# The second batch's attention moved ahead of most of the first batch's blocks, in a strided-attention and two-layer expert kernel

## Chip, cores and metric

One core of a Trainium2 chip runs the whole program once. The metric is device time in microseconds of that core.

## What is computed

```python
scores = scale * np.matmul(q, k.transpose(0, 1, 3, 2))     # 2 batches, 8 heads, 576 positions, 64 wide
mask_local = (rel >= 0) & (rel < 32)                       # heads 0 to 3
mask_strided = (rel >= 0) & (pos[None, :] % 32 == pos[:, None] % 32)   # heads 4 to 7
attn = softmax(np.where(masks, scores, -1e9))
x = (attn @ v)                                             # reshaped to 1152 tokens x 512
x = ((x @ w1) * (x @ w2)) @ w3 @ w_out                     # 512 -> 1024 -> 1024 -> 512
out = sum(p[:, e:e + 1] * (np.maximum(x @ e1[e], 0) @ e2[e]) for e in range(4))
```

## The kernel before

Matrices that TensorE multiplies are kept as a high and a low part, and a product is three matmuls (`mm3`, lines 247 to 249: high by high, low by high, high by low). The order of all instructions is written out by hand; each engine works through its own list in order.

**Attention** of one batch is six chunks, three local and three strided (`Chunk4`), taken in nine pipelined steps by `attend(b, s)`. In step s TensorE makes the scores of chunk s (lines 323 and 328, or 332 and 339), VectorE takes maxima and subtracts (345, 348), ScalarE exponentiates (354). VectorE sums and normalises chunk s - 1 (360 to 365). TensorE transposes chunk s - 2 (370), ScalarE evacuates it (375). TensorE multiplies chunk s - 3 by the values (387, 396), ScalarE writes x_hi (`put`, line 423) and VectorE x_lo (`put_lo`, line 427). In the first batch `keep_warm(12)` (line 118) puts twelve idle matmuls behind each step.

**Blocks.** `ab_block(b, ft, n)` computes one unit: half a batch (288 tokens) by 128 columns of both w1 and w2. That is two accumulators of 24 matmuls together; ScalarE copies the first (444), VectorE multiplies by the second (446), ScalarE and VectorE split the product into ab_hi and ab_lo (448, 450). There are 2 batches x 8 column groups x 2 halves = 32 units, and `units` lists them in order. Accumulators, transposes and outputs of the values share a pool of five PSUM banks (`ps`); scores have three of their own.

**Weights** come as 64-bit words in 20 chunks of 1 MB (8 of w1 and w2, 4 of w_out, 8 of w3), through two raw buffers. A generator, `work()`, converts one chunk in four steps that `advance(n)` takes one by one: clamp (147) with the split of the chunk before on ScalarE (164); split on VectorE (174) and shift (150); ScalarE's conversion of the next raw chunk (136) and the sign (153); ScalarE's magnitude of the next (144) and the add (157). Behind the add the raw buffer is free and SP issues the next load (`load_next`, line 132). `live` counts the 16 tiles that values and converted chunks share; a w1/w2 chunk gives its two back when the second half of the second batch has used it.

**Order before.** The first batch's nine steps run alone, with two worker steps at the end of each from step 4 on. Then come the first batch's 16 units, each with two worker steps, and behind nine of them one step of the second batch's attention. Then come the second batch's 16 units, and behind them the product of w3 with w_out (`wc_tile`), the product with the blocks and the experts, none of which the change touches.

Of the kernel before, what the change touches and what calls it, by code (L numbers as in the profile page):

```python
# [16 lines left out]
B, H, S, D = 2, 8, 576, 64  # L17
# [25 lines left out]
def kernel(  # L43
# [148 lines left out]
    def load_next():  # L192
        nonlocal loaded
        if loaded < len(stream):
            stream[loaded].raw_load()
            loaded += 1
# [40 lines left out]
    def advance(n=1):  # L237

        return all([next(worker, False) for _ in range(n)])

    def need(c, part=0):
        while not (c.done if part == 0 else c.done1 if part == 1 else c.done2):
            assert advance()
# [12 lines left out]
    def load_qk(b, g, cut=0):  # L256

        tq, tk = (big[b].tile([P, 2, S], F32, tag="big", name=name) for name in ("tq", "tk"))
        pairs = slice(2 * g, 2 * g + 2)
        for c in ([slice(0, cut), slice(cut, S)] if cut else [slice(0, S)]):  # L260
            for t, src, queue in ((tk, kT, nc.sync), (tq, qT, nc.scalar if cut else nc.sync)):
                queue.dma_start(out=t[:, :, c], in_=src[b, pairs, :, c].rearrange("k p n -> p k n"))
        qk[b, g] = (tq, tk)

    def load_v_loc(b, c):

        tv = wp.tile([P, 2, 3, P], F32, tag="w", name="tv_loc")

        def load(dst, rows, t0, n):
            nc.sync.dma_start(out=dst, in_=v_loc[b, :, rows, t0:t0 + n].rearrange("k p t d -> p k t d"))  # L270

        lower, upper, middle = slice(0, 64), slice(64, P), slice(W, 3 * W)
        if c == 0:
            load(tv[lower, :, 0:1], lower, 0, 1)
            load(tv[upper, :, 0:1], middle, 0, 1)
            load(tv[:, :, 1:], slice(0, P), 1, 2)
        elif c == 1:
            load(tv, slice(0, P), 3, 3)
        else:
            load(tv[lower, :, 0:1], lower, 0, 1)  # L280
            load(tv[upper], middle, 3, 3)
            load(tv[lower, :, 1:], middle, 1, 2)
        vals[b, 0, c] = tv

    def load_v_str(b):

        threes = [wp.tile([P, n, P], F32, tag="w", name="tv_str") for n in (8, 4)]
        for tv, t0, n in ((threes[0], 0, 4), (threes[1], 4, 1)):
            for k in range(2):
                nc.sync.dma_start(out=tv[64 * k:64 * k + T3, :2 * n].rearrange("p (h t) d -> p h t d", h=2),  # L290
                                in_=v_str[b, k, :2 * T3, t0:t0 + n].rearrange("(h p) t d -> p h t d", h=2))
        for k in range(2):
            nc.sync.dma_start(out=threes[1][64 * k:64 * k + NB, 2:], in_=v_str[b, k, 2 * T3:2 * T3 + NB, :2])
        vals[b, 1] = threes
# [137 lines left out]
    def ab_block(b, ft, n):  # L432
        t = slice(b * S + n * HB, b * S + n * HB + HB)
        if n == 0 and ft % 2 == 0:
            ab_hi[b, ft // 2] = big[b].tile([P, 2, S], F32R, tag="big", name="ab_hi")
            ab_lo[b, ft // 2] = big[b].tile([P, 2, S], F32R, tag="big", name="ab_lo")
        hi, lo = (x[b, ft // 2][:, ft % 2, n * HB:n * HB + HB] for x in (ab_hi, ab_lo))
        ab = tmp.tile([P, HB], F32, tag="pT", name="ab")
        for w in range(2):
            acc = bank("ab_acc")[:, :HB]  # L440
            for k in range(4):
                mm3(acc, c_w12[ft].parts((w * 4 + k) * P, P), (x_hi[:, k, t], x_lo[:, k, t]), k == 0, k == 3)
            if w == 0:
                nc.scalar.copy(ab, acc)
            else:
                nc.vector.tensor_tensor(out=ab, in0=acc, in1=ab, op=ALU.mult)
            yield
        nc.scalar.copy(hi, ab)
        yield
        nc.vector.tensor_tensor(out=lo, in0=ab, in1=hi.bitcast(F32), op=ALU.subtract)  # L450
        yield
# [224 lines left out]
    def load_probs():  # L676
        den = const.tile([P, NTT], F32, name="den")
        nc.sync.dma_start(out=pn, in_=probs)
        nc.vector.tensor_reduce(out=den, in_=pn, axis=mybir.AxisListType.X, op=ALU.add)
        nc.vector.tensor_scalar_add(den, den, 1e-9)  # L680
        nc.vector.reciprocal(den, den)
        nc.vector.tensor_tensor(out=pn, in0=pn, in1=den.unsqueeze(2).to_broadcast([P, NTT, E]), op=ALU.mult)
# [4 lines left out]
    with tc.manual_schedule():  # L687
# [9 lines left out]
        strided_masks()  # L697
        load_v_loc(0, 0)
        load_qk(0, 1)
        load_next()  # L700
        load_v_loc(0, 1)
        load_v_loc(0, 2)
        load_v_str(0)
        load_next()
        load_qk(1, 0)
        for c in range(3):
            load_v_loc(1, c)
        chunks = [[Chunk4(3 * g + c, b, g, c) for g in range(2) for c in range(3)] for b in range(B)]
        units = [(b, ft, i) for b in range(B) for ft in range(8) for i in range(2)]
        done = 0  # L710

        rest = iter(())
# [1 line left out]
        def run_unit():  # L714

            nonlocal done, rest
            b, ft, i = units[done]
            need(c_w12[ft])
            block = ab_block(b, ft, i)
            for _ in range(2):  # L720
                next(rest, None)
                next(block)
                advance(1)
            rest = block
            done += 1
            if b == i == 1:
                c_w12[ft].free()

        def attend(b, s):

            nonlocal live
            chunk = chunks[b]
            n = len(chunk)
            if s < n:
                chunk[s].scores()
                chunk[s].maxima()
                chunk[s].exps()
            if 1 <= s <= n:
                chunk[s - 1].sums()
                chunk[s - 1].normalise()  # L740
            if 2 <= s < n + 2:
                chunk[s - 2].transposes()
                chunk[s - 2].evac(nc.scalar.copy)
            if 3 <= s:
                c = chunk[s - 3]
                c.pv()
                c.put()
                c.put_lo()
                if c.g == 0 or c.c > 0:
                    live -= 1  # L750

        for s in range(9):
            attend(0, s)
            keep_warm(12)
            if s > 3:
                advance(2)
        load_qk(1, 1)
        load_v_str(1)
        steps = iter(range(9))
        while done < 16:  # L760
            run_unit()
            if done in (2, 4, 5, 7, 8, 10, 11, 13, 14):
                attend(1, next(steps))
        load_probs()
        while done < 32:
            run_unit()
        for _ in rest:
            pass
# [4 lines left out]
        for it in range(8):  # L773
# [8 lines left out]
            i = {1: 0, 3: 1, 6: 2}.get(it)  # L782
# [32 lines left out]
        for c in wc[:3]:  # L815
# [6 lines left out]
        steps = [Step(half, e, c, c_e[16 * i + 4 * e + c])  # L822
                 for i, half in enumerate(halves) for e in range(E) for c in range(4)]
# [100 lines left out]
```

## Time and profile before

| | us |
|---|---|
| median of 2 runs | 645.09 (644.95 to 645.22) |
| profiled execution | 647.48 |
| its span | 645.7 |
| TensorE matmuls busy | 625.6 (97%) |
| VectorE busy | 455.9 (71%) |
| ScalarE busy | 265.2 (41%) |
| mean granted TensorE clock | 0.992 of full speed |

Busy TensorE time is the time in which a matmul is in the engine; matmuls overlap, so one that is listed at 0.29 us may follow the one before it after 0.13 us. A share over the whole span is a mean over stages with different limits, so the rows below are taken by stage.

### The profile page before, as it was taken

To read this page: it belongs to the slowest core of one execution; us is meant where nothing else is said; L and a number is where in the kernel's file an instruction comes from. 1 tells how busy PE (TensorE), PEld (TensorE's weight loads), DVE (VectorE), ACT (ScalarE), POOL (GpSimd) and SP (SyncE) were. 2 spreads that over 40 slices of the span, in tenths; PEclk is the share of its full clock that TensorE was granted. 3 is DMA by queue.
4 is the path that set the end of the run, shared out by engine and by line. 5 is a ranking of instruction groups with operands and counts; after the bars stand their busy time and mean duration, and the time that the engine had idled before them with its cause. 6 is when DMAs were issued, how large, how long until landed. Compare 5 with 4: busy or idle time off the path is not lost.

```text
span 645.7 us, 11487 instructions
## 1 busy us (share of the span) xinstructions
PE 625.6 (97%) x4712; PEld 570.3 (88%) x4712; DVE 455.9 (71%) x834; ACT 265.2 (41%) x464; POOL 4.3 (1%) x19
## 2 busy tenths in 40 slices
PE   8788898999999999999999999999999999999997
PEld 6578787999988999998899889998798989999996
DVE  5787998499875423777787787797876576665843
ACT  2546465467655322433333343334433333333321
POOL 2000000000000000000000000000000000000000
PEclk9889999999999999999999999999999999999999
DMA  9846131233543310233444344433478464656321
GB/s 291 245 159 214 66 132 67 67 130 131 171 155 132 125 49 24 66 131 148 177 151 176 131 191 163 168 131 143 183 242 331 162 246 153 222 184 239 131 65 66
DMA packets 28728, 99.45 MB, mean 154 GB/s; under 512 B 2652, under 2 KB 6740, under 8 KB 26116
## 3 DMA queue, kind: packets, MB, share of 16 engines
q1 hardware_dynamic: 28132, 98.14, 43.0%
q8 instruction: 37, 0.61, 0.4%
q10 hardware_dynamic: 544, 0.59, 0.3%
q14 instruction: 15, 0.12, 0.1%
HBM read 79.58 MB, written 19.14 MB: 153 GB/s over the span
## 4 chain that ended last, share of the span: by engine, by line
PE 84%; DVE 8%; DMA 3%; issue 2%; ACT 1%; DVEq 0%; SPq 0%; ACTq 0%
PE g_acc L247 10%; PE g_acc L248 10%; PE g_acc L249 10%; PE m_a L247 4%; PE m_a L249 4%; PE m_a L248 4%; PE ab_acc L249 4%; PE ab_acc L247 4%; PE ab_acc L248 3%; DMA raw<-in_w_dram 3%; PE x_acc L249 3%; PE x_acc L248 3%; PE x_acc L247 3%; PE m_b L248 3%; PE m_c L247 3%; PE m_b L249 3%
## 5 line engine op out<-in xcount | busy, mean ns | idle before, releaser
L596 ACT ACTIVATE h_hi<-u 128x320 fp32r<-128x320 f32 (+1 forms) x128 | 56.9, 445 | 188.5 <-DVE u L602 188.5
L247 PE MATMUL g_acc<-w_hi,h_hi 128*128 128x512 f32 (+1 forms) x296 | 114.3, 386 | 0.0
L248 PE MATMUL g_acc<-w_lo,h_hi 128*128 128x512 f32 (+1 forms) x296 | 114.2, 386 | 0.0
L249 PE MATMUL g_acc<-w_hi,h_lo 128*128 128x512 f32 (+1 forms) x296 | 113.7, 384 | 0.0
L247 PE MATMUL ab_acc<-x_hi,w_hi 128*128 128x288 f32 x256 | 78.0, 305 | 3.4 <-ACT w_hi L164 1.6
L602 DVE TENSOR_TENSOR u<-m_b,u 128x320 f32<-128x320 f32 (+1 forms) x96 | 40.7, 452 | 53.4 <-PE m_b L249 53.4
L535 DVE TENSOR_TENSOR w_lo<-raw,w_hi 128x768 fp32r<-128x768 f32 x64 | 69.4, 1084 | 12.0 <-ACT w_hi L533 12.0
L249 PE MATMUL ab_acc<-x_hi,w_lo 128*128 128x288 f32 x256 | 76.9, 300 | 0.9 <-DVE w_lo L174 0.9
L248 PE MATMUL ab_acc<-x_lo,w_hi 128*128 128x288 f32 x256 | 76.7, 299 | 0.1
L249 PEld LDWEIGHTS g_acc<-w_hi,h_lo 128*128 128x128 f32 x296 | 55.6, 188 | 11.6
L247 PEld LDWEIGHTS g_acc<-w_hi,h_hi 128*128 128x128 f32 x296 | 55.8, 188 | 8.0
L248 PEld LDWEIGHTS g_acc<-w_lo,h_hi 128*128 128x128 f32 x296 | 55.7, 188 | 7.6
L598 DVE SCALAR_TENSOR_TENSOR h_lo<-u,h_hi 128x320 fp32r<-128x320 f32 (+1 forms) x128 | 57.5, 450 | 3.5 <-ACT h_hi L596 1.7
L533 ACT CAST w_hi<-raw 128x768 fp32r<-128x768 f32 x64 | 59.9, 936 | 0.0
L247 PEld LDWEIGHTS ab_acc<-x_hi,w_hi 128*128 128x128 f32 x256 | 49.2, 192 | 4.6 <-ACT x_hi L423 1.8
L249 PEld LDWEIGHTS ab_acc<-x_hi,w_lo 128*128 128x128 f32 x256 | 49.2, 192 | 1.4 <-DVE w_lo L174 1.4
L248 PEld LDWEIGHTS ab_acc<-x_lo,w_hi 128*128 128x128 f32 x256 | 49.3, 193 | 0.3 <-DVE x_lo L427 0.3
L136 ACT ACTIVATE raw<-raw 128x1024 int32<-128x1024 uint32 x20 | 23.2, 1162 | 37.4 <-DMA raw<-in_w3T_dram 20.0
L248 PE MATMUL m_b<-b_t,s_hi 128*128 128x320 f32 (+1 forms) x128 | 37.9, 296 | 0.0
L602 DVE TENSOR_TENSOR u<-m_a,u 128x320 f32<-128x320 f32 (+1 forms) x64 | 28.8, 451 | 11.4 <-PE m_a L249 11.4
L535 DVE TENSOR_TENSOR s_lo<-raw,s_hi 128x1024 fp32r<-128x1024 f32 x16 | 19.6, 1225 | 23.2 <-ACT s_hi L533 23.2
L602 DVE TENSOR_TENSOR u<-m_c,u 128x320 f32<-128x320 f32 (+1 forms) x64 | 28.9, 452 | 4.5 <-PE m_c L249 3.8
(148 smaller groups left out, 1395.1 us busy)
## 6 DMA issues: line engine op xcount, KB each, us to landing
raw<-in_e_dram SPq DMA_DIRECT2D x32, 1024.0 KB
raw<-in_w_dram SPq DMA_DIRECT2D x8, 1024.0 KB
raw<-in_w3T_dram SPq DMA_DIRECT2D x8, 1024.0 KB
stored<-s_hi SPq DMA_DIRECT2D x16, 512.0 KB
stored<-s_lo SPq DMA_DIRECT2D x16, 512.0 KB
s_hi<-stored SPq DMA_DIRECT2D x16, 512.0 KB
s_lo<-stored SPq DMA_DIRECT2D x16, 512.0 KB
raw<-in_w_out_dram SPq DMA_DIRECT2D x4, 1024.0 KB
```

What stands on the lines that cost most here:

```text
L136: nc.scalar.activation(self.low, self.low.bitcast(U32), AF.Copy, scale=2.0 ** -29)
L247: mm(acc, lh, rh, start=first, stop=False)
L248: mm(acc, lh, rl, start=False, stop=False)
L249: mm(acc, ll, rh, start=False, stop=last)
L533: nc.scalar.copy(dst[0], src)
L535: nc.vector.tensor_tensor(out=dst[1], in0=src, in1=dst[0].bitcast(F32), op=ALU.subtract)
L596: nc.scalar.activation(hi, src, AF.Relu)
L598: nc.vector.scalar_tensor_tensor(out=lo, in0=src, scalar=0.0, in1=hi.bitcast(F32), op0=ALU.max, op1=ALU.subtract)
L602: nc.vector.tensor_tensor(out=out, in0=acc, in1=b, op=ALU.add)
```

## The change

The second batch's attention follows directly on the first one's. Each step of `attend` now stops ahead of `put_lo`, and what stands between steps (idle matmuls and worker steps in the first batch; one unit, or a single worker step, in the second) is issued ahead of the x_lo writes. Four units stand in the second attention, at steps 1, 3, 5 and 7: the first batch's column groups 0 and 1. The units are listed anew: groups 0 and 1 of the first batch, then of the second, and from group 2 on both batches in turn, so that a later chunk serves four units in a row. The first weight chunk is loaded behind the values of local chunks 1 and 2 in place of ahead of them.

```diff
         load_qk(0, 1)
-        load_next()
         load_v_loc(0, 1)
         load_v_loc(0, 2)
+        load_next()
         load_v_str(0)
...
-        units = [(b, ft, i) for b in range(B) for ft in range(8) for i in range(2)]
+
+        units = [(b, ft, i) for b in range(B) for ft in range(2) for i in range(2)]
+        units += [(b, ft, i) for ft in range(2, 8) for b in range(B) for i in range(2)]
...
                 c.pv()
                 c.put()
+                yield
                 c.put_lo()
...
         for s in range(9):
-            attend(0, s)
+            step = attend(0, s)
+            next(step, None)
             keep_warm(12)
             if s > 3:
                 advance(2)
+            next(step, None)
         load_qk(1, 1)
         load_v_str(1)
-        steps = iter(range(9))
-        while done < 16:
-            run_unit()
-            if done in (2, 4, 5, 7, 8, 10, 11, 13, 14):
-                attend(1, next(steps))
+        for s in range(9):
+            step = attend(1, s)
+            next(step, None)
+            if s % 2:
+                run_unit()
+            else:
+                advance(1)
+            next(step, None)
         load_probs()
-        while done < 32:
+        while done < len(units):
             run_unit()
```

TensorE, at the end of the first batch's attention, before: the last idle matmul, and then the first unit's three products.

```order
L118 LDWEIGHTS idle
L118 MATMUL idle<-idle 128x256
L247 MATMUL ab_acc<-x_hi,w_hi 128x288
L248 MATMUL ab_acc<-x_lo,w_hi 128x288
L249 MATMUL ab_acc<-x_hi,w_lo 128x288
```

The same place on TensorE now (sc are scores, tq and tk the second batch's q and k).

```order
L118 MATMUL idle<-idle 128x256
L323 LDWEIGHTS i_loc
L323 MATMUL sc<-m_loc,i_loc 128x384
L328 MATMUL sc<-tk,tq 32x64 x24
L323 LDWEIGHTS i_loc
L323 MATMUL sc<-m_loc,i_loc 128x384
L328 MATMUL sc<-tk,tq 32x64 x24
L247 MATMUL ab_acc<-x_hi,w_hi 128x288
L248 MATMUL ab_acc<-x_lo,w_hi 128x288
L249 MATMUL ab_acc<-x_hi,w_lo 128x288
```

The scores of two of the second batch's chunks have moved ahead of the first unit.

VectorE, in the last steps of the first batch's attention (t and raw belong to weight chunks, x_lo to the output of the attention); lines with - stand there before, with + now.

```order
 L365 TENSOR_TENSOR p_pair<-p_pair,rec 128x8x54
+L157 ISA t<-raw_204,t 128x2048
+L147 TENSOR_SCALAR t<-t 128x1024
 L427 TENSOR_TENSOR x_lo<-o,x_hi 128x6x18 x4
-L157 ISA t<-raw_198,t 128x2048
-L147 TENSOR_SCALAR t<-t 128x1024
+L174 TENSOR_TENSOR w_lo<-t,w_hi 128x1024
+L150 TENSOR_SCALAR t<-t 128x1024
+L153 SCALAR_TENSOR_TENSOR t<-raw_214,t 128x1024
```

The add of the first chunk (157), behind which its raw buffer is free, has moved from behind four x_lo writes to ahead of them.

VectorE, between two steps of the second batch's attention (from the normalisation of one to the maximum of the next).

```order
 L365 TENSOR_TENSOR p_pair<-p_pair,rec 128x384
-L174 TENSOR_TENSOR w_lo<-t,w_hi 128x1024
-L150 TENSOR_SCALAR t<-t 128x1024
-L450 TENSOR_TENSOR ab_lo<-ab,ab_hi 128x288
-L446 TENSOR_TENSOR ab<-ab_acc,ab 128x288
-L153 SCALAR_TENSOR_TENSOR t<-raw_831,t 128x1024
+L153 SCALAR_TENSOR_TENSOR t<-raw_661,t 128x1024
+L446 TENSOR_TENSOR ab<-ab_acc,ab 128x288
+L157 ISA t<-raw_661,t 128x2048
 L345 TENSOR_REDUCE mx<-sc 128x6
```

Less of the blocks' and weights' work stands between the two steps than before.

## Rows read from the trace of the kernel before

**Rows 1.** Busy time by stage: stretch, length, PE, PEld, DVE, ACT, POOL, PEclk, DMA share, GB/s.

```profile
38.20:60.00 21.80, 20.08 (x217) 18.76 (x215) 17.62 (x27) 11.21 (x20) 0.00 (x0) 0.92 0.64 207
60.00:109.30 49.30, 43.19 (x632) 39.50 (x630) 45.05 (x91) 29.60 (x62) 0.00 (x0) 1.00 0.29 100
109.30:169.10 59.80, 58.86 (x432) 58.62 (x433) 47.51 (x74) 33.81 (x55) 0.00 (x0) 0.97 0.33 110
169.10:645.70 476.60, 471.78 (x2810) 428.85 (x2808) 320.81 (x589) 175.97 (x300) 0.00 (x0) 1.00 0.43 155
```

**Rows 2.** Time line, ends of the block stage and two units: start, length, engine, line, operation.

```profile
38.22 0.38 PE L247 MATMUL ab_acc<-x_hi,w_hi 128*128 128x288 f32 x1
...
126.44 0.40 ACT L444 COPY ab<-ab_acc 128x288 f32<-128x288 f32 x1 [0.64 <-PE ab_acc L249]
...
129.62 0.40 ACT L444 COPY ab<-ab_acc 128x288 f32<-128x288 f32 x1 [0.66 <-PE ab_acc L249]
...
169.13 0.39 PE L247 MATMUL wc_acc<-w_hi 128*128 128x512 f32 x1
```

**Rows 3.** Time line of VectorE in the second batch's attention.

```profile
61.13 0.55 DVE L345 TENSOR_REDUCE mx<-sc 128x6 f32<-128x384 f32 x1
...
63.67 1.22 DVE L174 TENSOR_TENSOR w_lo<-t,w_hi 128x1024 fp32r<-128x1024 f32 x1
64.81 0.69 DVE L150 TENSOR_SCALAR t<-t 128x1024 int32<-128x1024 int32 x1
65.41 0.45 DVE L450 TENSOR_TENSOR ab_lo<-ab,ab_hi 128x288 fp32r<-128x288 f32 x1
65.78 0.45 DVE L446 TENSOR_TENSOR ab<-ab_acc,ab 128x288 f32<-128x288 f32 x1
...
91.70 0.60 DVE L345 TENSOR_REDUCE mx<-sc 128x8 f32<-128x432 f32 x1
...
94.45 0.62 DVE L427 TENSOR_TENSOR x_lo<-o,x_hi 128x192 fp32r<-128x192 f32 x2
94.98 0.68 DVE L147 TENSOR_SCALAR t<-t 128x1024 f32<-128x1024 f32 x1
...
99.65 1.16 DVE L427 TENSOR_TENSOR x_lo<-o,x_hi 128x108 fp32r<-128x108 f32 x4
100.71 1.22 DVE L153 SCALAR_TENSOR_TENSOR t<-raw,t 128x1024 int32<-128x1024 int32 x1
```

**Rows 4.** Time line: the third weight chunk's load (SP's queue), what precedes and follows it.

```profile
32.31 1.09 DVE L427 TENSOR_TENSOR x_lo<-o,x_hi 128x108 fp32r<-128x108 f32 x4
...
33.32 1.21 DVE L157 CUSTOM_DVE_ANT_0 t<-raw,t 128x2048 uint16<-128x2048 uint16 x1
...
34.61 8.87 SPq L132 DMA_DIRECT2D raw<-in_w_dram  x2
...
39.58 1.19 ACT L136 ACTIVATE raw<-raw 128x1024 int32<-128x1024 uint32 x1 [2.69 <-DMA raw<-in_w_dram]
...
41.09 1.15 ACT L144 ACTIVATE t<-raw 128x1024 f32<-128x1024 f32 x1
```

**Rows 5.** Two gaps of TensorE in the time line, and four stretches by busy time.

```profile
20.89 0.67 PE L387 MATMUL o<-pT,tv_loc 64*64 64x32 f32 x33 [2.18 <-issue]
...
41.09 0.40 PE L247 MATMUL ab_acc<-x_hi,w_hi 128*128 128x288 f32 x1 [1.60 <-ACT x_hi L423]
...
22.00:24.00 2.00, 2.00 (x11) 1.41 (x10) 1.86 (x4) 1.20 (x2) 0.00 (x0) 0.50 0.95 320
42.00:44.00 2.00, 2.00 (x11) 2.00 (x10) 1.67 (x2) 1.15 (x2) 0.00 (x0) 0.50 0.00 0
62.00:64.00 2.00, 0.19 (x2) 0.20 (x3) 1.90 (x6) 1.70 (x4) 0.00 (x0) 1.00 0.04 12
78.00:80.00 2.00, 0.38 (x3) 0.31 (x3) 0.77 (x3) 2.00 (x6) 0.00 (x0) 1.00 0.00 0
```

## Prediction, made before the changed kernel ran

> **What bounds the kernel now.** I read first the share of busy time by stage, then the time line at the two ends of the block stage, then the waits inside it. From 169.1 us to the end TensorE is busy 471.78 of 476.60 us at full clock [rows 1]; the change touches nothing there, and in the order of the changed kernel the instructions from there on stand as before. So the end moves by as much as the start of that last stage moves. Ahead of it lies the block stage, from the first w1/w2 matmul at 38.22 us to the first w3 matmul at 169.13 us [rows 2], 130.9 us. It has two limits. From 60 to 109.3 us VectorE is busy 45.05 of 49.30 us, since the second batch's attention, the first batch's blocks and the weight chunks all go through it, and TensorE stands still for 6.1 us. From 109.3 to 169.1 us TensorE is busy 58.86 of 59.80 us and VectorE has a fifth of the time free [rows 1]. Over the three rows of the block stage TensorE is idle 1.72 + 6.11 + 0.94 = 8.8 us, and the mean granted clock of 0.92 over 21.8 us and 0.97 over 59.8 us takes about 1.7 + 1.8 = 3.5 us more [rows 1]. What is left, 130.9 - 8.8 - 3.5 = 118.6 us, is work. A unit of the blocks lasts 129.62 - 126.44 = 3.18 us on ScalarE's copies, one per unit [rows 2]; 32 of them are 101.8 us, which leaves 16.8 us for the second attention on TensorE. The change can therefore win at most 12.3 us here, 1.9% of the whole. I count 2% (12.9 us) as what a measurement tells from no change.
>
> **The change part by part.** It neither adds nor removes arithmetic; it moves it. What was spread over 13 units of the first batch (the second attention) now runs with only four units between its nine steps, so that it is bound by VectorE alone, and 28 units are left for a stretch that TensorE bounds. The question is how long TensorE stands idle in the first stretch, against 12.3 us lost before.
>
> When it starts. The write of x_lo now follows two steps of the weight worker. Four of these writes, 32.31 to 33.32 us, went before the add that frees the first raw buffer; now they go behind it, so the load that VectorE releases at 34.61 us starts 1.0 us sooner, and so does what waits for it: ScalarE's conversion at 39.58 and magnitude at 41.09 us (1.15 long) [rows 4]. The clamp behind the magnitude then starts at 42.24 - 1.0 = 41.2 us, and with 0.6 for it and 0.8 for the last x_lo writes of the first batch the second attention's first maximum starts at 42.6 us on VectorE. TensorE meets x later too: its first unit now stands behind two blocks of scores, so these cover the wait for x of 1.60 us at 41.09 us [rows 5].
>
> What VectorE then has to do, by start to start in the trace [rows 3]. A local chunk from maximum to normalise is 63.67 - 61.13 = 2.54 us, a strided one 94.45 - 91.70 = 2.75 us: 3 x 2.54 + 3 x 2.75 = 15.9. The x_lo writes are 94.98 - 94.45 = 0.53 us for a local and up to 100.71 - 99.65 = 1.06 us for a strided chunk: 3 x 0.53 + 3 x 1.06 = 4.8. The worker is called 13 times (five single steps and four units of two): 4 splits at 64.81 - 63.67 = 1.14, 4 shifts at 65.41 - 64.81 = 0.60, 3 signs and 3 adds taken like the splits (the add's own row has the same 1.21 us [rows 4]), 3 clamps taken like the shifts: 4.56 + 2.4 + 3.42 + 3.42 + 1.8 = 15.6. Of the four units 4 products and 3 subtractions at 0.37 (65.78 - 65.41) are 2.6. Together 38.8 us, so the last x_lo lands at 42.6 + 38.8 = 81.4 us if VectorE never waits. TensorE's own work in that time is 16.8 + 4 x 3.18 = 29.5 us.
>
> Where VectorE may wait. (a) The x_lo write is last in a step, and it frees the PSUM banks of the five that the next unit takes. Before the fourth unit's product VectorE has only an add and a subtraction left, 1.5 us: if both accumulators wait for the write, it stands 3.18 - 1.5 = 1.7 us, if only the second, 0.1 us. The order gives only the second a wait on VectorE; I take 0.1. (b) A unit may meet a halved clock. Twice 3.18 is 3.2 us more, four times 12.8 us; below, nothing, since before each product VectorE has more than 3.18 us of other work except in (a). I take 1.3, nearer to nothing, as the clock was halved in two of the four sparse stretches shown and full in the others [rows 5]. (c) ScalarE waits in order for each raw weight. A raw chunk and the strided q, k and v of this batch are now loaded from about 40 us on; the strided scores come at about 53 us by the sum above. Bounds 0 and the 5.0 us that a raw load took alone (34.61 to 39.58 us); I take 0, as these 2.8 MB (1.0, 1.2 and 0.6) at the 207 GB/s of that stretch [rows 1] need 13.5 us, 40 to 53.5. So x_lo is complete at 81.4 + 0.1 + 1.3 = 82.8 us.
>
> From there TensorE has 28 units, less the six matmuls of the first that need only the local heads, 0.8 us: 28 x 3.18 - 0.8 = 88.2 us. It comes out of a sparse stretch, so I add one fall of the clock, 1.7 us as above; without it 0. VectorE covers this: four units bring two chunks at 4.6 us and 2.9 us of products, 12.1 us against 12.7 us; if that cover goes, TensorE waits for what is over. The end is 82.8 + 88.2 + 1.7 = 172.7 us, against 169.13: 3.6 us later. The reason in one line: TensorE's lost time rises from 12.3 us to some 16, since 13 us of idle time are now collected in one stretch where VectorE alone has work.
>
> The first loads. The values go ahead of the first weight chunk. No wait names them, and the chunk is first read in the fifth of the nine steps, so I cost this at nothing. TensorE stood 2.18 us in the first batch's attention with no releaser (20.89 us), then ran at half clock from 22 to 24 us [rows 5]. Whether that gap recurs under another order of loads is open: bounds 3 us less and 3 us more, taken 0.
>
> The profiled execution took 647.48 us, of which 645.7 are the span; the median of the runs is 645.09. With 3.6 us the profiled one would be 651.1 and the median 648.7, which I predict.
>
> **A rule against the change.** After 1.81 us of idle time (62 to 64 us) the clock stayed at 1.00, yet at 42 to 44 us, behind a gap of 1.6 us and a few matmuls, it was 0.50 [rows 5]. The Trainium skill, "TensorE: Matmul & The Clock Gate", section "HAM oscillation — how this bites in real kernels", says that a kernel which computes in short bursts between waits finds its array at half rate again at every burst. By that rule all four units, and the local and strided scores with them, would run slow. The trace bears it out in part only.
>
> **Rivals.** A, slower: the sparse stretch is cold throughout. Its place is the four units at the odd steps; each costs 3.2 us more and VectorE stands for all of it: 12.8 in place of 1.3, 648.7 + 11.5 = 660.2 us. It decides once two in a row run cold. For it: five of the nine steps hold no unit. Against it: units have cover. Chance 0.08. B, a small gain: the early gap of TensorE goes with the new order of loads (3 us), the clock does not fall at 82 us (1.7) and no unit is cold (1.3): 648.7 - 6.0 = 642.7 us. For it: SP no longer stands behind the first weight chunk. Chance 0.24. C, the bunched loads arrive late and ScalarE holds up the exponentials: 648.7 + 5.0 = 653.7 us. Chance 0.12. D, that the idle time goes altogether and nothing takes its place, ends at 645.1 - 12.3 = 632.8 us; the sum of VectorE speaks against it. Chance 0.02. The forecast has 0.54.
>
> **How the numbers follow.** The range reaches to B below and past C above: 642.5 to 655.5 us, leaving out A, D and tails, under 2 in 10. Faster by over 2% is D, 0.02. Slower by over 2% is A, 0.08. Within 2% holds the rest, 0.90.
>
> **What would show it.** VectorE over 90% busy from about 43 to 82 us and TensorE near two thirds; the first w3 matmul at 172 to 173 us; 28 units in an unbroken row at 3.18 us behind 83 us. A lower mean clock between 45 and 80 us with VectorE waiting for the product of a unit would show A; ScalarE waiting for raw in that stretch, C. If the w3 matmuls start before 168 us, the sum of VectorE or the early gap was wrong; if TensorE waits after 85 us, the cover of the weights was.

## The result and the profile after

The changed kernel took 653.39 us (median of two runs, 653.37 to 653.41) against 645.09 us before: 8.3 us more, a ratio of 1.0118 with an interval of 1.0070 to 1.0166. That is slower, by less than the 2% that count here as a difference, and 4.7 us above the forecast of 648.7 us.

The profiled execution took 653.41 us with a span of 651.6 us. Its busy time by stage answers to [rows 1]. The columns are stretch, length, PE, PEld, DVE, ACT, POOL, granted clock, DMA share, GB/s. The first row ends where the second batch's attention begins on VectorE, the next two are that attention, the fourth is the unbroken row of blocks, and the last is from the w3 matmuls on.

```profile
35.30:39.88 4.58, 3.56 (x108) 2.71 (x106) 3.36 (x8) 3.60 (x7) 0.00 (x0) 1.00 0.29 79
39.88:60.00 20.12, 15.66 (x262) 13.57 (x261) 17.89 (x35) 8.37 (x15) 0.00 (x0) 0.75 0.48 176
60.00:85.70 25.70, 18.40 (x246) 16.59 (x246) 19.89 (x44) 13.07 (x30) 0.00 (x0) 0.80 0.27 85
85.70:174.90 89.20, 89.20 (x663) 89.20 (x663) 72.38 (x112) 53.39 (x87) 0.00 (x0) 0.98 0.38 129
174.90:651.60 476.70, 471.89 (x2812) 429.06 (x2810) 316.30 (x583) 172.97 (x295) 0.00 (x0) 1.00 0.42 151
```

The last stage is unchanged, 476.70 us against 476.60, so the end again moves with the first w3 matmul. In the row of blocks TensorE is busy 89.20 of 89.20 us. The extra time stands in the two rows between: in 45.82 us TensorE is busy 34.06 us (74%) at a clock of 0.75 and 0.80, and VectorE, the engine that was to bound this stretch, is busy only 37.78 us (82%).

VectorE's time line shows where the other 18% went: the clamp (L147) and the last x_lo writes stand ahead of the attention, the maximum of the first chunk begins it, and three of the four products of a unit (L446) stand waiting for TensorE.

```profile
38.53 0.69 DVE L147 TENSOR_SCALAR t<-t 128x1024 f32<-128x1024 f32 x1 [1.22 <-ACT t L144]
...
39.88 0.54 DVE L345 TENSOR_REDUCE mx<-sc 128x6 f32<-128x384 f32 x1
...
46.35 0.45 DVE L446 TENSOR_TENSOR ab<-ab_acc,ab 128x288 f32<-128x288 f32 x1
...
57.61 0.46 DVE L446 TENSOR_TENSOR ab<-ab_acc,ab 128x288 f32<-128x288 f32 x1 [1.79 <-PE ab_acc L249]
...
70.51 0.46 DVE L446 TENSOR_TENSOR ab<-ab_acc,ab 128x288 f32<-128x288 f32 x1 [2.63 <-PE ab_acc L249]
...
81.29 0.46 DVE L446 TENSOR_TENSOR ab<-ab_acc,ab 128x288 f32<-128x288 f32 x1 [2.80 <-PE ab_acc L249]
...
85.66 0.19 DVE L679 TENSOR_REDUCE den<-pn 128x9 f32<-128x36 f32 x1
```

From 39.88 us to the first operation that is no longer the attention's (L679) are 45.8 us. The waits are 1.79 + 2.63 + 2.80 = 7.2 us, so the work is 38.6 us.

TensorE's time line shows why VectorE waited. Read the start of one block matmul to the next: 0.24 us apart is half clock, 0.13 us is full.

```profile
45.35 0.90 PE L370 MATMUL tp<-ident,p_pair 128*128 128x128 f32 x3 [2.21 <-DVE p_pair L365]
...
50.53 0.90 PE L370 MATMUL tp<-ident,p_pair 128*128 128x128 f32 x3 [2.25 <-DVE p_pair L365]
51.36 1.51 PE L387 MATMUL o<-pT,tv_loc 64*64 64x32 f32 x48
52.80 0.61 PE L247 MATMUL ab_acc<-x_hi,w_hi 128*128 128x288 f32 x1
53.20 0.44 PE L248 MATMUL ab_acc<-x_lo,w_hi 128*128 128x288 f32 x1
53.44 0.44 PE L249 MATMUL ab_acc<-x_hi,w_lo 128*128 128x288 f32 x1
...
57.08 0.29 PE L248 MATMUL ab_acc<-x_lo,w_hi 128*128 128x288 f32 x1
57.22 0.29 PE L249 MATMUL ab_acc<-x_hi,w_lo 128*128 128x288 f32 x1
57.35 0.36 PE L332 MATMUL sc<-m_str,i_str 128*128 128x432 bf16 x1
...
62.63 1.09 PE L370 MATMUL tp<-ident,p_pair 128*128 128x128 f32 x4 [1.56 <-DVE p_pair L365]
...
65.09 0.61 PE L247 MATMUL ab_acc<-x_hi,w_hi 128*128 128x288 f32 x1
...
70.24 0.60 PE L370 MATMUL tp<-ident,p_pair 128*128 128x128 f32 x4
...
74.98 0.63 PE L370 MATMUL tp<-ident,p_pair 128*128 128x128 f32 x4 [3.28 <-DVE p_pair L365]
...
76.28 0.61 PE L247 MATMUL ab_acc<-x_hi,w_hi 128*128 128x288 f32 x1
...
81.11 0.81 PE L396 MATMUL o<-pT,tv_str 54*64 54x54 f32 x32
...
85.44 0.41 PE L248 MATMUL ab_acc<-x_lo,w_hi 128*128 128x288 f32 x1 [2.40 <-DVE x_lo L427]
...
175.20 0.39 PE L247 MATMUL wc_acc<-w_hi 128*128 128x512 f32 x1
```

TensorE stands 1.6 to 3.3 us for the normalised scores, which VectorE delivers, and then the unit begins at half clock. The three units that do so are called cold here, and one at full clock warm. The cold ones take 57.35 - 52.80 = 4.6, 70.24 - 65.09 = 5.2 and 81.11 - 76.28 = 4.8 us, where a warm one takes 3.18 [rows 2]. One can read a loop in this: a cold unit makes VectorE late, VectorE makes the next normalised scores late, and TensorE stands idle again. The rows show each wait, not that one brings on the next. The granted clock in 4-us stretches shows the same falls:

```profile
48.00:52.00 4.00, 1.75 (x33) 1.25 (x35) 3.83 (x9) 1.84 (x3) 0.00 (x0) 0.50 0.72 252
52.00:56.00 4.00, 4.00 (x49) 3.94 (x43) 3.72 (x8) 1.70 (x5) 0.00 (x0) 0.55 0.04 14
...
64.00:68.00 4.00, 4.00 (x56) 3.94 (x53) 3.74 (x9) 1.81 (x5) 0.00 (x0) 0.50 0.79 256
...
76.00:80.00 4.00, 3.94 (x33) 3.81 (x26) 2.48 (x6) 1.79 (x6) 0.00 (x0) 0.57 0.27 33
```

What full clock would have given can be worked out from these rows. The three units are longer than 3.18 us by 1.4, 2.0 and 1.6 us; taken off the waits of 1.79, 2.63 and 2.80 us that leaves 0.4, 0.6 and 1.2 us. So some 5 of the 7.2 us come of the units' clock, and about 2.2 of what stands ahead of them: the matmuls before the unit, cold too (the products at 51.36 us take 1.51 us), and the place of the unit. This was worked out, and the experiments test it.

### The profile page after: what moved, and what is told of

Its sections match the earlier page's. It is cut to its first block, busy times and chain, and to the rows that moved or that the text cites. A ratio compares the mean times of both kernels' runs of the same rounds, so it can differ in the third digit from the quotient of the medians.

```text
span 651.6 us, 11462 instructions
## 1 busy us (share of the span) xinstructions
PE 629.0 (97%) x4712; PEld 575.0 (88%) x4712; DVE 455.9 (70%) x834; ACT 265.9 (41%) x464; POOL 4.2 (1%) x19
## 4 chain that ended last, share of the span: by engine, by line
PE 89%; DVE 7%; DMA 1%; ACT 1%; issue 1%; DVEq 0%; SPq 0%
PE g_acc L247 10%; PE g_acc L248 10%; PE g_acc L249 10%; PE ab_acc L247 5%; PE ab_acc L248 5%; PE ab_acc L249 5%; PE m_a L247 4%; PE m_a L249 4%; PE m_a L248 4%; PE x_acc L249 3%; PE x_acc L248 3%; PE x_acc L247 3%; PE m_b L248 3%; PE m_c L247 3%; PE m_b L247 3%; PE m_c L248 3%
## 5 line engine op out<-in xcount | busy, mean ns | idle before, releaser
L248 PE MATMUL ab_acc<-x_lo,w_hi 128*128 128x288 f32 x256 | 78.3, 306 | 3.4 <-DVE x_lo L427 3.4
L248 PEld LDWEIGHTS ab_acc<-x_lo,w_hi 128*128 128x128 f32 x256 | 50.7, 198 | 3.9 <-DVE x_lo L427 3.9
L247 PEld LDWEIGHTS ab_acc<-x_hi,w_hi 128*128 128x128 f32 x256 | 50.8, 198 | 0.4 <-ACT pT L375 0.2
L249 PEld LDWEIGHTS ab_acc<-x_hi,w_lo 128*128 128x128 f32 x256 | 50.6, 198 | 0.0
```

What stands on the lines that cost most here:

```text
L247: mm(acc, lh, rh, start=first, stop=False)
L248: mm(acc, lh, rl, start=False, stop=False)
L249: mm(acc, ll, rh, start=False, stop=last)
```

## The experiments

The theory at the outset: the halved clock in the sparse stretch, fed by the gaps between the steps, makes the cold units late, and VectorE loses 7.2 us on them. The rivals: the place of the unit (it stands ahead of its step's x_lo write, which frees banks of the pool that units take from); the new order of the first loads; and too few blocks between the steps, whatever the clock. All ratios below are to the kernel before, run beside it on the same chip. "Waits for products" are those of L446 for TensorE from the first maximum of the second attention to L679.

**Idle matmuls behind every step of the second attention.** They compute nothing that is used, but take TensorE's time and one bank of the shared pool of five.

```diff
             else:
                 advance(1)
+            keep_warm(12)
             next(step, None)
         load_probs()
```

> The changed kernel with twelve idle matmuls behind the work of each step of the second attention, as the first attention has them. Theory 1 (clock): VectorE waits 7.2 us for products of units because units two to four start at half clock; kept warm, a unit takes 3.18 us again, the waits shrink to about 1 us (the fourth unit's) and the fall of the clock behind the stretch goes too, so 6 to 8 us less than the changed kernel, 645 to 647 us, granted clock over 0.95 from 40 to 80 us. Theory 2 (place): VectorE waits because the unit stands behind the transposes and values of its step, whatever the clock; then the idle matmuls lie in front of the scores and change nothing or cost up to 4 us, 653 to 657 us, though the clock is up.

Measured: 650.47 us (648.21 to 652.50, four runs), ratio 1.0088 [1.0054, 1.0122]. The busy time of 36 to 88 us, first of the changed kernel, then of this one:

```profile
36.00:88.00 52.00, 39.22 (x606) 34.74 (x595) 42.64 (x89) 26.40 (x55) 0.00 (x0) 0.79 0.34 117
```

```profile
36.00:88.00 52.00, 46.52 (x748) 41.13 (x737) 45.78 (x95) 29.20 (x58) 0.00 (x0) 1.00 0.37 121
```

The clock goes from 0.79 to 1.00. VectorE's waits in the same window, from the view of waits (in total, times, longest):

```profile
DVE ab L446 <- ACT t L144: 1.6, 1, 1.6
...
DVE ab L446 <- ACT ab L444: 1.0, 2, 0.5
DVE ab L446 <- PE ab_acc L249: 0.6, 1, 0.6
```

The last of these lies behind the end of the attention:

```profile
82.05 0.18 DVE L679 TENSOR_REDUCE den<-pn 128x9 f32<-128x36 f32 x1
...
87.60 0.46 DVE L446 TENSOR_TENSOR ab<-ab_acc,ab 128x288 f32<-128x288 f32 x1 [0.64 <-PE ab_acc L249]
```

So within the attention the wait for TensorE falls from 7.2 us to nothing, and 3.1 us of waits for ScalarE (2.6 of products, 0.5 of a split) take part of its place. The attention lasts 82.05 - 40.24 = 41.8 us, and without these 38.7, the same work as in the changed kernel. The first w3 matmul moves from 175.20 to 170.00 us. In these traces, then, the waits hang on the clock. What the clock is worth in timed runs is not shown: the time lies between the two ranges that were expected, the profiled execution was the fastest of the four, the interval overlaps that of the changed kernel, and 650.47 - 644.88 = 5.6 us of the loss remain at the median, in which the price of the idle matmuls cannot be told from the rest.

**The order of the first loads**, alone and undone. The first kernel is the changed one with the old order, the second the kernel before with the new order and nothing else.

```diff
+        load_next()
         load_v_loc(0, 1)
         load_v_loc(0, 2)
-        load_next()
```

> The changed kernel with the first weight chunk loaded ahead of the values of chunks 1 and 2 again, as before. If the order of loads ended TensorE's early gap of 2.18 us, the gap comes back and with the cold stretch behind it the first attention ends some 3 us later: 655 to 657 us. If the gap is an accident of the one profiled execution of the kernel before, the time stays at 653 us.

> The kernel before with only the order of the first loads changed. If the order of loads ends the early gap, 642 to 643 us; if the gap stood in the profiled execution alone (647.48 against a median of 645.09), no change from the kernel before, 645 us.

Measured: 654.21 us with the old order, ratio 1.0152 [1.0125, 1.0180], between the two expectations and without a stop of 2 us in its profile (the longest is 0.91 us); 645.23 us for the kernel before with the new order, 1.0021 [0.9995, 1.0047]. The load order did not make the loss; at most the new order saves some 0.3% in the changed kernel, and the intervals overlap. The second kernel also gives a profile of the old schedule without the 2.18 us gap of [rows 5]:

```profile
35.63 0.38 PE L247 MATMUL ab_acc<-x_hi,w_hi 128*128 128x288 f32 x1
...
166.48 0.39 PE L247 MATMUL wc_acc<-w_hi 128*128 128x512 f32 x1
```

Its first unit is 38.22 - 35.63 = 2.6 us earlier than in [rows 2], and its first w3 matmul 169.13 - 166.48 = 2.65 us: in these two profiles of the old schedule the early loss goes through to the end undiminished. Against this profile the change moved the w3 matmul by 175.20 - 166.48 = 8.7 us, close to the 8.3 us of the medians.

**A unit in each of eight steps** instead of in four, the first four groups of the first batch going first so that only its own x is needed.

```diff
-        units = [(b, ft, i) for b in range(B) for ft in range(2) for i in range(2)]
-        units += [(b, ft, i) for ft in range(2, 8) for b in range(B) for i in range(2)]
+        units = [(b, ft, i) for b in range(B) for ft in range(4) for i in range(2)]
+        units += [(b, ft, i) for ft in range(4, 8) for b in range(B) for i in range(2)]
...
-            if s % 2:
+            if s:
                 run_unit()
```

> The changed kernel with a unit in each of steps 1 to 8 of the second attention (eight in place of four, groups 0 to 3 of the first batch), the rest of the list as in the change. TensorE then has 16.8 + 8 x 3.18 = 42.2 us of work there, VectorE 38.6 + 4 x 0.73 for products + 4 more worker steps at about 1.0 = 45.5 us. Theory 1: dense work in every step keeps the clock up, waits for products go, the stretch ends near 86 us with 24 units left instead of 28: 12.7 us less than the changed kernel by the units and about as late an end of the attention, 638 to 642 us. Theory 2: every unit makes VectorE wait 2 to 3 us, eight of them 20 us, the stretch ends near 105 us: 652 to 660 us.

Measured: 644.63 us (640.97 to 647.31, ten runs), ratio 0.9994 [0.9968, 1.0020]. With eight blocks between the steps the loss is gone, at a clock of 0.93 in 36 to 88 us and 2.9 us of waits for products (2.17 and 0.68). The time lies between the two ranges expected. The edit changes three things, the share of dense work, how it is spread, and the worker's steps in the stretch (17 in place of 13), so the next one spreads the same work.

**Half a unit in each of eight steps.** The same four units as in the change, one accumulator (12 matmuls) to a step; the worker's single step remains behind the first step of the attention only, as in the kernel above, so it takes 9 steps there instead of 13.

```diff
+        def half_unit(s):
+            nonlocal done, rest, block
+            if s % 2:
+                b, ft, i = units[done]
+                need(c_w12[ft])
+                block = ab_block(b, ft, i)
+            next(rest, None)
+            next(block)
+            advance(1)
+            if s % 2 == 0:
+                rest = block
+                done += 1
+
+        block = None
...
-            if s % 2:
-                run_unit()
+            if s:
+                half_unit(s)
             else:
                 advance(1)
```

> The changed kernel with its four units cut in half: one accumulator (1.6 us) in each of steps 1 to 8 of the second attention, no single worker steps but in step 0. Theory 1 (clock): the dense work per step is still thin, so the clock still falls, but a half at half clock is 1.6 us longer and has a whole step of VectorE's other work before its product: the waits for products (7.2 us in the changed kernel) fall below 3 us and the time to 648 to 651 us, although the granted clock from 44 to 84 us stays near 0.8. Theory 2 (place): the same sum of work stands behind the same transposes, the waits stay and the time is 652 to 655 us.

Measured: 642.86 us (641.22 to 646.76, seven runs), ratio 0.9949 [0.9919, 0.9980]. This beats both kernels, and both ranges that were expected: 0.5% under the one before, and its interval lies well below that of the changed one. Busy time of the attention and of the 28 units behind it:

```profile
36.00:88.00 52.00, 46.51 (x720) 41.43 (x718) 47.18 (x98) 30.57 (x63) 0.00 (x0) 0.94 0.37 122
74.80:162.80 88.00, 88.00 (x665) 88.00 (x665) 77.12 (x117) 55.58 (x90) 0.00 (x0) 1.00 0.42 143
```

The second half of the first unit on TensorE, and its product on VectorE:

```profile
45.35 0.47 PE L247 MATMUL ab_acc<-x_hi,w_hi 128*128 128x288 f32 x1
...
48.01 0.44 PE L249 MATMUL ab_acc<-x_hi,w_lo 128*128 128x288 f32 x1
...
48.59 0.45 DVE L446 TENSOR_TENSOR ab<-ab_acc,ab 128x288 f32<-128x288 f32 x1
```

No idle matmul was added, yet the clock, which was expected to stay near 0.8, is 0.94, and 1.00 in every 4-us stretch from 52 us on. VectorE waits 1.2 us for products. Its attention runs from 39.58 to 74.81 us, 35.2 us against 45.8, and from there to the first w3 matmul are 162.80 - 74.81 = 88.0 us where the changed kernel took 175.20 - 85.66 = 89.5: the fall of the clock behind the sparse stretch is gone too. The edit does three things: it lays the blocks evenly, it takes four worker steps out of the stretch, and it puts a unit's product one step later on VectorE, so that more of VectorE's work lies ahead of it. The last shows in the first unit: its second half is cold from 45.35 us to its end, 0.24 us from matmul to matmul, and its product at 48.59 us waits for nothing. What the worker steps are worth is parted from the other two below; the even clock and the later product are not parted by any run.

**Eight units with idle matmuls** behind the steps that had shown gaps.

```diff
             else:
                 advance(1)
+            if s in (1, 5, 6, 8):
+                keep_warm(8)
             next(step, None)
```

(on the kernel with eight units)

> Eight units as in the run of that name, with eight idle matmuls (0.9 us at full clock) behind steps 1, 5, 6 and 8, where that run's TensorE waited 2.2, 0.7 to 1.2 and 1.8 us and the clock fell after it. Theory 1: the three cold stretches of that run (about 1.7 us each, and the 4.1 us that VectorE waited for products) go at a price of up to 3.6 us for the idle matmuls: 638 to 642 us, faster than the kernel before. Theory 2: the stretch is bound by the sums of VectorE and TensorE, and the idle matmuls are only added work: 645 to 648 us.

Measured: 647.31 us, ratio 1.0015 [0.9999, 1.0031]. The clock stays where it was, 0.93, the waits for products are not fewer (4.8 us against 2.9), and ScalarE waits 7.6 us for VectorE's subtraction. The attention ends at 94.06 us, against 88.82 in the profile without them. Here the idle matmuls bought no clock; that they cost time is not shown, since the two intervals overlap.

**The x_lo write ahead of the unit.** The step no longer stops before the write, so the banks that the unit takes come free sooner.

```diff
                 c.put()
-                yield
                 c.put_lo()
                 if c.g == 0 or c.c > 0:
                     live -= 1
+                yield
```

> The changed kernel with the x_lo writes back at the head, ahead of the unit, the worker steps and the idle matmuls (in both attentions). Theory 1: the banks come free some 2 us sooner but the units still start behind the normalisation at half clock: VectorE's waits for products stay at 5 to 9 us and the time within 3 us of the changed kernel's 653 us. Theory 2 (place): units wait for banks that the late x_lo writes hold; freed sooner, the waits fall below 3 us and the time to 646 to 649 us.

Measured: 650.40 us (646.64 to 651.20, nine runs), ratio 1.0057 [1.0029, 1.0085]. The waits for products fall from 7.2 to 4.2 us while the clock stays low, 0.80. Neither expectation holds as a whole: the time lies at the edge of the first one's, the waits between the two. The 4.2 us stand at the second and the fourth unit, which begin cold (2.21 and 1.95 us); the third, which runs warm from 65.29 to 68.56 us, makes VectorE wait for nothing. So the place is probably part of the loss, although the interval overlaps that of the changed kernel, and about half of the loss (0.57 of 1.18%) remains while two units are cold.

**Idle matmuls only at the end of the attention**, ahead of the row of blocks.

```diff
+        keep_warm(24)
         load_probs()
```

> The changed kernel with 24 idle matmuls (2.7 us) between the second attention and the 24 remaining groups of matmuls of the first unit after it. If the fall of the clock behind the attention is worth 1.7 us, the w3 matmuls start 1 to 2 us earlier than in the changed kernel's profile (175.2 us); if the idle matmuls only push the unit back, 0 to 2 us later.

Measured: 652.97 us in one run, w3 at 174.75 us. TensorE no longer stands idle for the last x_lo, and from 85.49 us to the w3 matmuls the clock is 1.00. From the end of the attention to the first w3 matmul are 174.75 - 86.76 = 88.0 us, against 175.20 - 85.66 = 89.5 in the changed kernel, 1.5 us less, which fits a fall of the clock worth 1.7; but the attention itself ended 1.1 us later. One run, 0.45 us: not told from no change.

**What the even spread owes to what.** Four kernels side by side: the changed kernel again; the changed kernel without the worker's single steps behind steps 2, 4, 6 and 8 of the attention (9 worker steps); the half units with a second worker step there (13, as in the change, though in the change two stand behind each odd step and one behind each even step, and here it is the other way round); and the half units with 9 worker steps and the x_lo write ahead, by the edit shown above. The first diff is on the changed kernel, the second on the half units.

```diff
             if s % 2:
                 run_unit()
-            else:
+            elif s == 0:
                 advance(1)
```

```diff
             if s:
                 half_unit(s)
-            else:
+            if s % 2 == 0:
                 advance(1)
```

> The changed kernel once more, on the chip of the three above: 653 us, VectorE waiting 7 to 9 us for products, the clock halved in three of four units.

> The changed kernel with 9 worker steps in the second attention (the single ones of steps 2, 4, 6 and 8 left out; they follow later), its four units whole. Theory 1: VectorE's sum falls by 3.9 to 34.9 us, but the units stay cold and each product has less ahead of it, so the waits stay at 7 us or grow; 649 to 653 us. Theory 3: with 9 worker steps the whole gain of the halves is there, 642 to 645 us.

> The halves again, but with 13 worker steps in the second attention as in the changed kernel (a second one in steps 2, 4, 6 and 8) in place of 9. It differs from the changed kernel in one thing, where the dense work of four units stands. Theory 1 (clock): spread evenly the clock stays up, VectorE waits under 3 us for products, the attention lasts 38.8 us plus that, the w3 matmuls start at 166 to 168 us and the time is 645 to 647 us, 6 to 8 below the changed kernel. Theory 3 (worker steps): the gain of the halves came from four worker steps that left the stretch; put back, the time is the changed kernel's, 651 to 654 us.

> The halves (9 worker steps) with the x_lo writes at the head again, ahead of the half unit and the worker steps. That alone made the changed kernel 3 us faster; if the banks that come free sooner count here too, 640 to 642 us; if it only made up for cold units, no change from the halves' 643 us.

| kernel | us | ratio to before | waits for products, us | clock 36 to 88 us | first w3, us |
|---|---|---|---|---|---|
| changed, again | 653.63 | 1.0112 [1.0087, 1.0138] | 6.8 | 0.81 | 175.08 |
| changed, 9 worker steps | 651.46 | 1.0082 [1.0052, 1.0112] | 9.2 | 0.84 | 172.50 |
| half units, 13 worker steps | 648.59 | 1.0047 [1.0024, 1.0070] | 2.3 | 0.87 | 169.95 |
| half units, 9 worker steps, x_lo ahead | 643.08 | 0.9957 [0.9931, 0.9982] | 0.3 | 0.93 | 163.71 |

The rows behind it, the busy time of 36 to 88 us of the second, and of the third:

```profile
36.00:88.00 52.00, 39.87 (x641) 35.43 (x640) 40.14 (x88) 25.00 (x53) 0.00 (x0) 0.84 0.28 97
```

```profile
36.00:88.00 52.00, 42.80 (x666) 37.45 (x665) 45.65 (x95) 29.23 (x58) 0.00 (x0) 0.87 0.36 121
```

And the wait that the second one gathers (in total, times, longest), the longest single wait for a product in these traces among them:

```profile
DVE ab L446 <- PE ab_acc L249: 9.2, 3, 4.2
```

With whole units and four fewer worker steps the attention lasts 84.49 - 40.09 = 44.4 us; less 9.2 us of waits for products and 1.1 for ScalarE that is 34.1 us of work in place of 38.6, but the attention is only 0.8 us shorter than the 85.53 - 40.30 = 45.2 us of the first row, since VectorE waits longer. This came as the first theory expected. Cutting and spreading the blocks, with all 13 worker steps, takes 653.63 - 648.59 = 5.0 us off and cuts the waits from 6.8 to 2.3 us; the intervals of these two lie apart. It missed both expectations, 645 to 647 and 651 to 654 us: the stretch still loses its clock once, 0.50 in 64 to 68 us, and the half that is cold there (67.07 to 69.98 us) makes its product wait 2.30 us. Only with the blocks spread do the four worker steps pay in full: from 1.0047 to 0.9949 (the half units above) or 0.9957. Apart, the two edits give 2.2 and 5.0 us; together some 10. Why they help each other is left open; one row points at the x_lo write. With 13 worker steps two of them (59.11 and 60.36 us) stand ahead of such a write, and TensorE waits 1.86 us for it before the next half (61.99 us), behind which the clock falls; with 9 the same wait is 0.26 us, and the clock over 36 to 88 us is 0.94 in place of 0.87. With the half units the place of the x_lo write makes no difference (0.9949 and 0.9957).

## Why the prediction was right in sign and short in size

**What bounds the end, and that the end moves by the start of the w3 stage.** Right: 476.60 and 476.70 us.

**When it starts: 42.6 us.** It was 39.88 us, by the path that was named: raw load, ScalarE's magnitude, the clamp at 38.53 us that waits for it, the last x_lo writes, the first maximum. The base had taken the profiled execution of before with its 2.18 us gap and the half clock behind it [rows 5]; that execution was 2.6 us late by its first unit, as the run with the new loads shows, and 42.6 - 2.6 = 40.0. The profile after did not have this loss. No load order is shown to bring the gap: the changed kernel under the old order has no stop at that place, and the kernel before gained nothing from the new one. As the median was taken from the profiled time by their own difference, the error did not reach the 648.7 us; it hides a part of the next one when the two profiles are laid side by side.

**VectorE's sum: 38.8 us.** Measured 38.6. Durations taken from rows of before, counted by the steps in the code, held to 0.2 us.

**Waits (a) and (b): 0.1 and 1.3 us.** This is the step that went wrong: the term for cold units was priced at 1.3 us, and the waits were 7.2 us together, inside the bounds of 0.1 to 1.7 and 0 to 12.8, but far from the end that was chosen. The reason given was that the clock had been halved in two of four sparse stretches before. Those two at full clock, 62 to 64 and 78 to 80 us [rows 5], lay in a stretch in which TensorE was busy 43.19 of 49.30 us [rows 1]; the changed kernel's attention has it busy 34.06 of 45.82 us, with units at every other step, and three of four began cold. The second reason, that VectorE has more than 3.18 us of other work ahead of each product, leaves out when the unit may begin: it stands on TensorE behind a step's transposes and products, which wait for VectorE. So the cover, that is VectorE's other work, begins to be used up before the unit starts. The Trainium skill, "TensorE: Matmul & The Clock Gate", section "HAM oscillation — how this bites in real kernels", says of a kernel whose short bursts of matmuls stand between longer waits for loads that every burst finds the array at half rate again. What it says of bursts, which the prediction counted as borne out in part, was nearer to the changed kernel's trace: three of four units began at half clock. But they stand behind gaps of 1.6 to 3.3 us in which TensorE waited for VectorE, shorter than the units themselves, so the page's case is not this one.

**Rival A, cold throughout, 660.2 us.** Its mechanism was the one that happened, in the place it named, with a chance of 0.08; its price was too high. It had VectorE pay 3.2 us for each of four units. The sign named for the forecast, VectorE over 90% busy, did not come (82%); A's sign did. One unit stayed warm, and the other three warmed up on the way (4.6 to 5.2 us in place of 6.4). That the measured 653.39 us still lies inside 642.5 to 655.5 us is luck as far as the mechanism goes: the upper end was set for rival C's late loads, which did not come, and A was left out of the range.

**(c) and rival C, late raw loads.** Did not happen, although C's 653.7 us lie next to the measured time: ScalarE waited 3.8 us for raw weights between 30 and 100 us, against 15.6 us in the same window before, and no wait of VectorE inside the attention names them. In the second profile of the changed kernel TensorE did wait 1.22 us for the strided q. Rival B's early gap is not shown to go with the load order, which gained nothing in the kernel before (1.0021), so its 3 us had no ground, and its two other parts, a clock that does not fall and no cold unit, are what the half units show, not the change. Rival D's idle time did not vanish.

**28 units in an unbroken row, 88.2 us, and one fall of the clock, 1.7.** Right: from the end of the attention to the first w3 matmul are 175.20 - 85.66 = 89.5 us, TensorE waits for nothing in the row, and the half units, which enter it warm, do it in 88.0.

Against the expected first w3 matmul of 172.7 us it came at 175.2: 2.7 us sooner by the start, 5.8 us later by the cold units and their place, the rest within 0.6 us. The one-line reason, that TensorE's idle time is collected in one stretch, holds, but lacks its second half: this stretch lost its clock as well (0.75 and 0.80), and then the engine that was thought to have time to spare made VectorE wait.

## What to carry to other kernels

When dense work is put between the steps of a chain on another engine, count not only how much of it there is but how it is spread: with the same number of worker steps, four blocks at every other step ran at a clock of 0.81 and the same four in halves at every step at 0.87; the cut, with the later products that it brings, was worth 5.0 us, and with fewer worker steps the halves came to 0.94. A unit that waits for the engine it is to feed is priced cold until a row shows it warm, and its cover counts only from the moment at which it can begin. Idle matmuls were the second choice here: behind whole units at every other step they raised the clock to 1.00 and showed no sure gain in the timed runs, and where dense work already stood in the steps they raised nothing.

## What the runs showed that was not expected

The half units, without a single idle matmul, held the clock at 0.94 in 36 to 88 us and at 1.00 from 52 us on, where the whole units had 0.79 to 0.84.

TensorE stops early with no releaser in every one of the fourteen traces, always at the same matmul of its list, three ahead of the end of the third local chunk's product (L387), but for 0.39 to 2.31 us: at 23.76 us the changed kernel stood 0.57 us, and in its second profile 2.31 us:

```profile
25.32 0.42 PE L387 MATMUL o<-pT,tv_loc 64*64 64x32 f32 x3 [2.31 <-issue]
```

Yet both took the same time (653.41 and 653.51 us), as the second attention began at 39.88 and 40.30 us: only 0.4 us of the longer stop remain. The stop of 2.18 us [rows 5] is another one: it stands 127 matmuls earlier in the list, in the trace of the kernel before alone, ahead of a maximum that VectorE then waited 1.66 us for, and there 2.6 us went through to the end. So the two do not show that either order of work bears a stop better. What stops TensorE at these places stays open. Over 16 to 21 runs the kernel before spreads by 5.3 to 6.7 us (643.13 to 649.16 us in one series), so that two runs that agree within 0.3 us say less of its median than they seem to.
